# The first loads, the first value products and the issue queue of a gated attention-and-MLP kernel, reordered

## The chip, the cores and the metric

One core of one Trainium2 chip. The metric is the time of one execution on the device, in microseconds (us); lower is better. The kernel before takes 156.6 us (median of three runs, 156.52 to 161.58). "PE" is the matmul engine, "DVE" the vector engine, "ACT" the activation engine, "POOL" the GpSimd engine and "SP" the engine that issues most DMAs; "PEld" in a view is PE's loading of weights. Times inside an execution are counted from the start of the profile's span, which is about 1.7 us shorter than the time of the run.

## The reference, cut to what matters

```python
x = A_x                                              # 1 x 2048 x 448, bf16
g = sigmoid((x * gate_w).sum(-1, keepdims=True))     # gate: one column of numbers
q, k, v = split(x @ wqkv)                            # 16 heads of 28
pq, pk = q @ w_phi, k @ w_phi                        # per head
phi = concat([softmax(p), softmax(-p)])              # for p in pq, pk
kv, z = phi_k^T v, sum(phi_k)
a = (phi_q kv / (phi_q z + 1e-6)) @ wo
b = gelu(x @ w1 + b1) @ w2 + b2                      # 448 -> 1792 -> 448
return g * a + (1 - g) * b
```

## The kernel before

The kernel keeps `x` transposed in `xT`, in four blocks of 512 tokens. Blocks 1 to 3 come transposed by the DMA (`load_x`). Block 0 is loaded plainly into `x0` and transposed by PE, so that PE has work early. `WvG` holds the value weights plus one column for the gate; its last 64 rows come by a small load of their own, called **the tail** below. `Wk` and `Wq` come through transposing loads and are fused with `w_phi` on PE ("fusions", tile `w_ps`), giving `Wpk` and `Wpq`. The tiles `xS`, `WqS`, `WkS` and `WvS` are copies with the two halves of the partitions swapped, made by SBUF-to-SBUF DMAs.

The first loads:

```python
warm = w2_sb[:, 0, :]
gate = w2_sb[:, 1, :]
nc.vector.memset(w2_sb[:, 0:2, :], 0.0)          # warm and gate in one
nc.vector.memset(wphi[64:P, 3, :], 0.0)
nc.vector.memset(WvG[0:64, 3, :], 0.0)
...
for m, eng in ((0, nc.scalar), (1, nc.sync)):     # x0: a half on each queue
    eng.dma_start(x0[:, 2*m:2*m+2, :], ...)
nc.scalar.dma_start(WvG[:, 0:3, 0:D], ...)
nc.scalar.dma_start(WvG[64:P, 3, 0:D], ...)       # the tail
nc.sync.dma_start(gate[0:1, :], gate_w[None, :])  # waits for the memset
nc.scalar.dma_start(wphi[:, 0:3, :], ...)
...
load_wT(WkT, D)        # SP, transposing; SP issues in order, so after the gate
load_wT(WqT, 0)
load_x(1)
```

The start of PE's program, and the queue of swaps:

```python
dummies(8)                      # warm the clock
turn_x0(0, xp[0]); turn_gate(); turn_x0(1, xp[1])
fill_bd()
v_pair(0, on_act=True); v_pair(1)
prep(WkT, wk_at, (1, 0, 1)); prep(WqT, wq_at, (1, 0, 0))     # fusions
# SP, in this order: b1, block 2, WqS, xS(0), block 3, WkS, xS(1), WvS, w1, wo
k_pair(0); k_pair(1); ...; k_pair(2); v_pair(2); ...; k_pair(3); v_pair(3, b1=True)
for g in range(NG): q_pair(g, 0)
```

All accumulators rotate through the eight PSUM banks: three buffers "pair" and one "acc", of two banks each. A tile made earlier or later shifts the rotation of all that follow.

Of the kernel before, what the change touches and what calls it, by code (L numbers as in the profile page):

```python
# [35 lines left out]
def kernel(  # L36
# [75 lines left out]
    nc.gpsimd.memset(b1c, 0.0)  # L112
    warm = w2_sb[:, 0, :]
    gate = w2_sb[:, 1, :]
    nc.vector.memset(w2_sb[:, 0:2, :], 0.0)  # L115
    nc.vector.memset(wphi[64:P, 3, :], 0.0)
# [3 lines left out]
    x0 = oT[:, 0, 0:4 * D].rearrange("p (t d) -> p t d", t=4)  # L120
    for m, eng in ((0, nc.scalar), (1, nc.sync)):
        eng.dma_start(x0[:, 2 * m:2 * m + 2, :],
                      x[m * 256:(m + 1) * 256, :].rearrange("(t p) d -> p t d", p=P))
    nc.scalar.dma_start(WvG[:, 0:3, 0:D],
                        A_wqkv[0:384, 2 * D:3 * D].rearrange("(c p) n -> p c n", p=P))
    nc.scalar.dma_start(WvG[64:P, 3, 0:D], A_wqkv[384:448, 2 * D:3 * D])
    nc.sync.dma_start(gate[0:1, :], gate_w[None, :])
    nc.scalar.dma_start(wphi[:, 0:3, :], wphi_rows[0:384, :].rearrange("(c p) b -> p c b", p=P))
# [6 lines left out]
    def load_wT(W, base):  # L135
        nc.sync.dma_start_transpose(W[:], A_wqkv[:, base:base + NC4 * P])
# [6 lines left out]

    load_wT(WkT, D)
    load_wT(WqT, 0)
    load_x(1)
    nc.scalar.dma_start(wphi[0:64, 3, :], wphi_rows[384:448, :])


    nc.gpsimd.memset(ident[:], 1.0)  # L150
    nc.gpsimd.affine_select(out=ident[:], in_=ident[:], pattern=[[-1, P]],
# [46 lines left out]

    def v_pair(u, on_act=False, b1=False):
        v_ps = four("v_ps")  # L200
        for i in range(2):
            t = 2 * u + i
            for c in range(NC4):
                nc.tensor.matmul(v_ps[:, i, 0:D + 1], lhsT=xT[:, c, t * P:(t + 1) * P],  # L204
                                 rhs=WvG[:, c, :], start=(c == 0), stop=(c == NC4 - 1))
        if b1:
            nc.tensor.matmul(v_ps[:, 1, 480:480 + NJ], lhsT=b1c, rhs=ident[:, 0:NJ],
                             start=True, stop=True, skip_group_check=True)
        v_out(u, v_ps, slice(2 * u, 2 * u + 2), on_act)
        if b1:  # L210
            nc.vector.tensor_copy(out=b1T[:], in_=v_ps[:, 1, 480:480 + NJ])
# [117 lines left out]
    def turn_x0(m, tp):  # L329
        for i in range(2):  # L330
            for c in range(NC4):
                lo = c * P if c < 3 else 320
                nc.tensor.transpose(tp[:, c, i * P:(i + 1) * P], x0[:, 2 * m + i, lo:lo + P],  # L333
                                    ident[:])
        copy(m == 1, xT[:, :, m * 256:(m + 1) * 256], tp[:])

    def turn_gate():
        g_ps = four("g_ps")
        for c in range(NC4):
            lo = c * P if c < 3 else 320  # L340
            nc.tensor.matmul(g_ps[:, 0, c:c + 1], lhsT=gate[:, lo:lo + P], rhs=ident[:, 0:1],
                             start=True, stop=True)
        nc.vector.tensor_copy(out=WvG[:, 0:3, D], in_=g_ps[:, 0, 0:3])
        nc.vector.tensor_copy(out=WvG[HP:P, 3, D:D + 1], in_=g_ps[HP:P, 0, 3:4])

    def dummies(n):
        w_ps = four("warm_ps")
        for _ in range(n):
            nc.tensor.matmul(w_ps[:, 0, 0:D], lhsT=warm[:, 0:P], rhs=warm, start=True, stop=True)  # L349


    dummies(8)
    xp = [ps.tile([P, NC4, 256], BF16, name="xp", tag="pair", bufs=3) for _ in range(2)]
    turn[0] += 2
    turn_x0(0, xp[0])
    turn_gate()
    turn_x0(1, xp[1])
    fill_bd()
    v_pair(0, on_act=True)
    v_pair(1)  # L360
    prep(WkT, wk_at, (1, 0, 1))
    prep(WqT, wq_at, (1, 0, 0))
    def swap_w(W_S, W):
        nc.sync.dma_start(W_S[0:HP, :, :], W[HP:P, :, :])
        nc.sync.dma_start(W_S[HP:P, 0:3, :], W[0:HP, 0:3, :])

    nc.sync.dma_start(b1c[0:NJ, :], B_b1.rearrange("(j p) -> j p", p=P))
    load_x(2)
    swap_w(WqS, Wpq)
    swap_x(0)  # L370
    load_x(3)
    swap_w(WkS, Wpk)
    swap_x(1)
    swap_w(WvS, WvG)
    for f in (slice(0, F // 2), slice(F // 2, F)):
# [10 lines left out]
    k_pair(2)  # L386
    v_pair(2)
    k_norm(1)
# [152 lines left out]
```

## Time and profile before

| | kernel before |
|---|---|
| runs | 156.6, 156.52, 161.58 us |
| span of the profile | 154.4 us |
| first transpose / first value product | 4.42 / 6.18 us |
| first fusion / first keys / first queries | 9.25 / 11.14 / 20.43 us |
| first hidden unit (`hp`) / first product of the queries with `kv` and `z` (`nm`) / first output (`y`) | 43.33 / 89.75 / 90.60 us |

The starts on PE are milestones: if one is later by as much as the next, nothing was gained or lost between. The prediction shows the views. Two lines of the issue queues that I passed over also belong here. They are from the timelines of SP and of ACT (start, length of the issue, queue, line, kind, what), and show Wk's transposing load and the tail:

```profile
1.81 2.40 SPq L136 DMA_TRANSPOSE WkT<-in_A_wqkv_dram  x1
```

```profile
1.87 0.53 ACTq L126 DMA_DIRECT2D WvG<-in_A_wqkv_dram  x1
```

The two are issued 0.06 us apart, on different queues.

### The profile page before, as it was taken

The numbers are of one execution on the slowest core, as the hardware profiler recorded it, in microseconds if no ns is written. First come the engines' busy times: TensorE is split into PE (matmuls) and PEld (weight loads), VectorE is DVE, ScalarE is ACT, GpSimd is POOL, SyncE is SP. The second block draws the span as 40 slices with busy tenths as digits, with TensorE's granted clock in tenths as the row PEclk, the third lists the DMA queues.
The fourth block names the chain that finished last, engine by engine and source line by source line (L and its number), as shares of the span: only waits on it lengthen the run. The fifth ranks groups of instructions, "written<-read, shape, count | busy, mean of one in ns | idle before, by whom it ended". The sixth has DMA issues, their size and how long they took to land.

```text
span 154.4 us, 3179 instructions
## 1 busy us (share of the span) xinstructions
PE 149.4 (97%) x1303; PEld 86.6 (56%) x1303; DVE 83.2 (54%) x245; ACT 76.5 (50%) x87; POOL 32.4 (21%) x35
## 2 busy tenths in 40 slices
PE   6999999999999999999999999999999999999991
PEld 2575578666666854444444455555556555555581
DVE  3364999388891050000000059999977999977100
ACT  0559759998889527776767640111311111111121
POOL 7920489929775000000000000000000000000000
PEclk9999999999999999999999999999999999999999
DMA  4999999999993000000000001114332124334401
GB/s 151 239 213 148 213 232 254 219 222 215 218 351 135 4 0 4 0 0 4 0 0 0 4 0 34 34 39 97 93 94 64 40 64 93 81 83 38 123 30 30
DMA packets 28270, 14.91 MB, mean 97 GB/s; under 512 B 20062, under 2 KB 27872, under 8 KB 28256
## 3 DMA queue, kind: packets, MB, share of 16 engines
q1 hardware_dynamic: 27024, 14.06, 41.5%
q10 hardware_dynamic: 1232, 0.66, 1.5%
q8 instruction: 10, 0.16, 0.4%
q14 instruction: 4, 0.03, 0.1%
HBM read 6.11 MB, written 1.84 MB: 51 GB/s over the span
## 4 chain that ended last, share of the span: by engine, by line
PE 96%; DVE 1%; ACT 0%; issue 0%; ACTq 0%
PE hp L421 27%; PE y L480 27%; PE pq L303 8%; PE y L486 8%; PE nm L436 4%; PE v_ps L204 4%; PE pk L273 4%; PE v_ps L287 4%; PE pk L295 3%; PE acc L314 2%; PE warm_ps L349 2%; PE w_ps L220 1%; PE xp L333 0%; DVE xT L192 0%; ACT res L489 0%; DVE w_sb L115 0%
## 5 line engine op out<-in xcount | busy, mean ns | idle before, releaser
L480 PE MATMUL y<-w_sb,gel 128*128 128x448 bf16 (+1 forms) x238 | 45.2, 341 | 0.0
L421 PE MATMUL hp<-xT,w_sb 64*128 64x512 bf16 x196 | 42.7, 376 | 0.0
L421 PE MATMUL hp<-xS,w_sb 64*128 64x512 bf16 x196 | 42.3, 376 | 0.0
L426 ACT ACTIVATE gel<-hp,b1T 128x1024 bf16<-128x1024 f32 x28 | 30.8, 1110 | 13.0 <-PE hp L421 13.0
L489 ACT ACTIVATE res<-y,ungate 128x448 bf16<-128x448 f32 (+1 forms) x17 | 10.4, 611 | 50.4 <-PE y L486 50.3
L480 PEld LDWEIGHTS <-gel 128*128 128x128 bf16 x238 | 23.1, 98 | 19.0
L421 PEld LDWEIGHTS <-w_sb 64*128 64x128 bf16 x392 | 20.6, 94 | 21.5
L264 POOL TENSOR_TENSOR phik<-phik,rec 128x1792 bf16<-128x1792 bf16 (+1 forms) x8 | 25.0, 3127 | 15.0 <-DVE rec L261 15.0
L441 DVE COPY st<-nm 128x32 f32<-128x32 f32 x32 | 4.5, 183 | 35.6 <-PE nm L436 35.6
L457 DVE TENSOR_TENSOR tmp<-nm,al 128x448 bf16<-128x448 f32 x32 | 18.4, 616 | 0.0
L259 DVE TENSOR_REDUCE sums<-phik 128x64 f32<-128x1792 bf16 x8 | 16.0, 2005 | 2.6 <-ACT phik L252 2.6
L486 PE MATMUL y<-wo_sb,oT 128*128 128x448 bf16 (+1 forms) x68 | 14.7, 341 | 0.0
L303 PE MATMUL pq<-xT,Wpq 64*128 64x512 bf16 x56 | 13.6, 376 | 0.0
L303 PE MATMUL pq<-xS,WqS 64*128 64x512 bf16 x56 | 12.0, 376 | 0.0
L192 DVE CAST vaug<-v_ps 128x896 bf16<-128x896 f32 x7 | 7.5, 1073 | 4.7 <-PE v_ps L287 3.2
L308 ACT ACTIVATE EqP<-pq 128x1024 bf16<-128x1024 f32 x8 | 8.3, 1040 | 3.4 <-PE pq L303 3.4
L309 ACT ACTIVATE EqN<-pq 128x1024 bf16<-128x1024 f32 x8 | 8.3, 1042 | 0.0
L436 PE MATMUL nm<-KVbd,EqP 128*128 128x120 bf16 x64 | 8.3, 216 | 0.0
L436 PE MATMUL nm<-KVbd,EqN 128*128 128x120 bf16 x64 | 8.3, 216 | 0.0
L251 ACT ACTIVATE phik<-pk 128x896 bf16<-128x896 f32 x8 | 7.5, 941 | 1.4 <-PE pk L273 1.4
L486 PEld LDWEIGHTS <-oT 128*128 128x128 bf16 x68 | 6.1, 98 | 3.3
L252 ACT ACTIVATE phik<-pk 128x896 bf16<-128x896 f32 x8 | 7.6, 949 | 0.0
(87 smaller groups left out, 147.7 us busy)
## 6 DMA issues: line engine op xcount, KB each, us to landing
w_sb<-in_B_w_dram SPq DMA_DIRECT2D x4, 784.0 KB, 14.2
out_dram<-res SPq DMA_DIRECT2D x15, 112.0 KB, 1.9
w_sb<-in_B_w_dram SPq DMA_DIRECT2D x1, 1568.0 KB, 17.4
xS<-xT SPq DMA_DIRECT2D x2, 256.0 KB, 4.0
xS<-xT SPq DMA_DIRECT2D x2, 192.0 KB, 4.3
WvG<-in_A_wqkv_dram ACTq DMA_DIRECT2D x1, 336.0 KB, 4.2
wo_sb<-in_A_wo_dram SPq DMA_DIRECT2D x1, 336.0 KB, 17.4
WqS<-Wpq SPq DMA_DIRECT2D x1, 256.0 KB, 4.2
```

The source lines that it names most:

```text
L259: nc.vector.reduce_sum(out=sums[:], in_=ph, axis=AX.X)
L264: eng.tensor_tensor(out=ph[:, lo:hi], in0=ph[:, lo:hi], in1=rec[:, lo:hi, :, None].to_broadcast([P, hi - lo, 2, DH]), op=ALU.mult)
L303: nc.tensor.matmul(pq[:, i, :], lhsT=w_half(Wpq, WqS, i, k)[:, g * P:(g + 1) * P], rhs=x_half(i, k, h), start=(k == 0), stop=(k == NK - 1))
L308: nc.scalar.activation(out=EqP[:, g, dst], in_=src, func=ACT.Exp)
L309: nc.scalar.activation(out=EqN[:, g, dst], in_=src, func=ACT.Exp, scale=-1.0)
L421: nc.tensor.matmul(hp[:, i, :], lhsT=w1_sb[i * HP:(i + 1) * HP, k, j * P:(j + 1) * P], rhs=x_half(i, k, h), start=(k == 0), stop=(k == NK ...
L426: nc.scalar.activation(out=gel[h][:, j, :], in_=hp[:].rearrange("p a b -> p (a b)"), func=ACT.Gelu_apprx_tanh, bias=b1T[:, j:j + 1])
L436: nc.tensor.matmul(nm[s][:, g * 2 * KW:(g + 1) * 2 * KW], lhsT=E[:, g, tok], rhs=KVbd[:, g, s, :], start=True, stop=True)
L457: nc.vector.tensor_tensor(out=tmp[:, s, :].rearrange("p (x h d) -> p x h d", x=NPR, h=2), in0=nmv[s][:, :, 0:PW].rearrange("p x (h d) -> p ...
L480: nc.tensor.matmul(y, lhsT=gel[t // 8][:, j, (t % 8) * P:(t % 8 + 1) * P], rhs=w2_sb[:, j, cols], start=(j == 0), stop=False)
L486: nc.tensor.matmul(y, lhsT=oT[:, c, tok], rhs=wo_sb[:, c, cols], start=False, stop=(c == NC4 - 1))
L489: nc.scalar.activation(out=res[:, cols], in_=y, func=ACT.Copy, scale=ungate[:, t:t + 1])
```

## The change

The intent is to feed the first value product sooner: half of `x0` and `Wv` go first, the rest of `x0` follows and is transposed inside the first value pair, block 1 is multiplied while `Wq` is still on its way, and `WvS` and `xS` are swapped earlier because nothing holds them up.

```diff
-    warm = w2_sb[:, 0, :]
+    warm = w2_sb[:, 0, 0:P]
-    nc.vector.memset(w2_sb[:, 0:2, :], 0.0)
+    nc.vector.memset(warm, 0.0)
+    nc.vector.memset(gate, 0.0)
...
-    for m, eng in ((0, nc.scalar), (1, nc.sync)):
-        eng.dma_start(x0[:, 2 * m:2 * m + 2, :], ...)
-    nc.scalar.dma_start(WvG[:, 0:3, 0:D], ...)
+    nc.scalar.dma_start(x0[:, 0:2, :], ...)
+    nc.sync.dma_start(WvG[:, 0:3, 0:D], ...)
     nc.scalar.dma_start(WvG[64:P, 3, 0:D], ...)
+    nc.scalar.dma_start(x0[:, 2:4, :], ...)
     nc.sync.dma_start(gate[0:1, :], gate_w[None, :])
...
     load_wT(WkT, D)
+    load_x(1)
     load_wT(WqT, 0)
-    load_x(1)
+    nc.scalar.activation(out=first[:], in_=warm[0:1, 0:1], func=ACT.Exp)
...  # gate casts from DVE to ACT; all copies of transposes on DVE;
...  # the dummies: one PSUM tile for all, 512 columns by repeating warm
-    dummies(8)
+    dummies(7)
     turn_x0(0, xp[0])
     turn_gate()
-    turn_x0(1, xp[1])
+    dummies(1)
+    v_pair(0, on_act=True, between=lambda: turn_x0(1, xp[1]))
     fill_bd()
-    v_pair(0, on_act=True)
     v_pair(1)
     prep(WkT, wk_at, (1, 0, 1))
+    v_pair(2)
     prep(WqT, wq_at, (1, 0, 0))
...
+    swap_w(WvS, WvG)
+    swap_x(0)
     load_x(2)
     swap_w(WqS, Wpq)
-    swap_x(0)
     load_x(3)
     swap_w(WkS, Wpk)
     swap_x(1)
-    swap_w(WvS, WvG)
...
     k_pair(2)
-    v_pair(2)
```

More of the change, by code (lines that the diff above doesn't have):

```diff
@@ L120 @@
     x0 = oT[:, 0, 0:4 * D].rearrange("p (t d) -> p t d", t=4)
-    for m, eng in ((0, nc.scalar), (1, nc.sync)):
-        eng.dma_start(x0[:, 2 * m:2 * m + 2, :],
-                      x[m * 256:(m + 1) * 256, :].rearrange("(t p) d -> p t d", p=P))
-    nc.scalar.dma_start(WvG[:, 0:3, 0:D],
-                        A_wqkv[0:384, 2 * D:3 * D].rearrange("(c p) n -> p c n", p=P))
+    nc.scalar.dma_start(x0[:, 0:2, :], x[0:256, :].rearrange("(t p) d -> p t d", p=P))
+    nc.sync.dma_start(WvG[:, 0:3, 0:D],
+                      A_wqkv[0:384, 2 * D:3 * D].rearrange("(c p) n -> p c n", p=P))
     nc.scalar.dma_start(WvG[64:P, 3, 0:D], A_wqkv[384:448, 2 * D:3 * D])
+    nc.scalar.dma_start(x0[:, 2:4, :], x[256:512, :].rearrange("(t p) d -> p t d", p=P))
     nc.sync.dma_start(gate[0:1, :], gate_w[None, :])
@@ L144 @@
     load_wT(WkT, D)
+    load_x(1)
     load_wT(WqT, 0)
-    load_x(1)
     nc.scalar.dma_start(wphi[0:64, 3, :], wphi_rows[384:448, :])
+    first = consts.tile([1, 1], F32, name="first")
+    nc.scalar.activation(out=first[:], in_=warm[0:1, 0:1], func=ACT.Exp)
     nc.gpsimd.memset(ident[:], 1.0)
@@ L197, in v_out, with v_pair @@
         copy(on_act, lg[:, tiles], v_ps[:, :, D])
-    def v_pair(u, on_act=False, b1=False):
+    def v_pair(u, on_act=False, b1=False, between=None):
         v_ps = four("v_ps")
@@ L202, in v_pair @@
             t = 2 * u + i
+            if i == 1 and between is not None:
+                between()
             for c in range(NC4):
@@ L334, in turn_x0 @@
                                     ident[:])
-        copy(m == 1, xT[:, :, m * 256:(m + 1) * 256], tp[:])
+        copy(False, xT[:, :, m * 256:(m + 1) * 256], tp[:])
     def turn_gate():
@@ L342, in turn_gate @@
                              start=True, stop=True)
-        nc.vector.tensor_copy(out=WvG[:, 0:3, D], in_=g_ps[:, 0, 0:3])
-        nc.vector.tensor_copy(out=WvG[HP:P, 3, D:D + 1], in_=g_ps[HP:P, 0, 3:4])
+        nc.scalar.copy(out=WvG[:, 0:3, D], in_=g_ps[:, 0, 0:3])
+        nc.scalar.copy(out=WvG[HP:P, 3, D:D + 1], in_=g_ps[HP:P, 0, 3:4])
+    w_ps = four("warm_ps")
     def dummies(n):
-        w_ps = four("warm_ps")
         for _ in range(n):
-            nc.tensor.matmul(w_ps[:, 0, 0:D], lhsT=warm[:, 0:P], rhs=warm, start=True, stop=True)
-    dummies(8)
+            nc.tensor.matmul(w_ps[:, 0, :], lhsT=warm, rhs=warm[:, None, :].to_broadcast([P, 4, P]),
+                             start=True, stop=True)
+    dummies(7)
     xp = [ps.tile([P, NC4, 256], BF16, name="xp", tag="pair", bufs=3) for _ in range(2)]
```

## The prediction

> **What bounds the kernel now.** First I read the page's busy shares and slices, then the chain that ended last, then the start of the timeline by engine, because everything the change moves lies before 29 us.
>
> The page of the kernel before: busy shares, then the slices.
>
> ```profile
> PE 149.4 (97%) x1303; PEld 86.6 (56%) x1303; DVE 83.2 (54%) x245; ACT 76.5 (50%) x87; POOL 32.4 (21%) x35
> ...
> DMA  4999999999993000000000001114332124334401
> ```
>
> The matmul engine PE is busy for 149.4 of 154.4 us, so at most 5 us of the span hold no matmul. The chain puts 96% on PE. DMA engines are full too, but only for the first 12 slices (to about 46 us). So whatever moves the time has to change PE's work, or its idle time, or its clock before the second product.
>
> The waits of PE, then its timeline up to the first query pair (start, length, engine, line, what, idle before it).
>
> ```profile
> PE warm_ps L349 <- DVE w_sb L115: 1.5, 1, 1.5
> PE v_ps L204 <- DVE WvG L343: 0.3, 1, 0.3
> ```
>
> ```profile
> 1.46 3.17 PE L349 MATMUL warm_ps<-w_sb 128*128 128x448 bf16 x8 [1.46 <-DVE w_sb L115]
> 4.42 0.89 PE L333 MATMUL xp<-ident,oT 128*128 128x128 bf16 x8
> ...
> 5.25 0.61 PE L333 MATMUL xp<-ident,oT 128*128 128x128 bf16 x8
> 6.18 3.04 PE L204 MATMUL v_ps<-WvG,xT 128*128 128x449 bf16 x15 [0.33 <-DVE WvG L343]
> ...
> 9.25 1.09 PE L220 MATMUL w_ps<-w_sb,WkT 128*128 128x140 bf16 x16
> 10.18 1.13 PE L220 MATMUL w_ps<-w_sb,WqT 128*128 128x140 bf16 x16
> 11.14 4.76 PE L273 MATMUL pk<-Wpk,xT 128*128 128x448 bf16 x24
> ...
> 20.43 0.39 PE L303 MATMUL pq<-xT,Wpq 64*128 64x512 bf16 x1
> ```
>
> PE's only waits are 1.46 us at the start and 0.33 us at 6.18; the rest of the 5 us is the tail after 151 us. From 6.18 on it streams: 16 value matmuls by 9.25 (0.192 us each), 16+16 fusions by 11.14 (0.059 each). No wait on x0's load shows, so loading it sooner gains nothing by itself.
>
> The second thing to see is the issue queue SP, which feeds PE from 20 us on.
>
> ```profile
> 13.54 0.57 SPq L364 DMA_DIRECT2D WqS<-Wpq  x1
> 14.15 1.06 SPq L365 DMA_DIRECT2D WqS<-Wpq  x1
> 15.26 0.65 SPq L141 DMA_DIRECT2D xS<-xT  x1
> 15.96 0.62 SPq L142 DMA_DIRECT2D xS<-xT  x1
> ...
> 23.00 0.90 SPq L364 DMA_DIRECT2D WvS<-WvG  x1
> 23.94 0.72 SPq L365 DMA_DIRECT2D WvS<-WvG  x1
> ```
>
> SP issues without a pause from 1.8 to 32 us. The tile view of xS gives up to 4.6 us from issue to landing: the copy issued at 15.96 lands at 20.52 by its completion records. The first query matmul that reads xS starts at 20.57. WvS, issued at 23.94 and 4.2 us under way, lands at 28.04 to 28.14; the first matmul that reads it starts at 28.15, though its partner started at 27.80. So the queue is just in time twice, and costs PE about 0.1 us at 20.5 and 0.35 us at 27.8.
>
> **What the Trainium skill says.**
> - "TensorE: Matmul & The Clock Gate", Part 1: PE runs at half clock until about 3.4 us of sustained activity, in a free-running window. The trace agrees: dummies of 448 columns are 0.373 us apart, later matmuls 0.19; the spacing of the transposes drops from 0.107 to 0.056 us at about 4.95, 3.5 us after PE's start.
> - The same page, Part 4, says transposes don't reach the full clock. The trace differs: the second eight are 0.055 us apart.
> - "VectorE: DVE Perf Modes", Zero memsets can be issued as uint32: one cycle per element whatever the width. The trace agrees: 448 elements 0.43 us, 224 0.24 us, 14 0.07 us.
> - "DMA: Bandwidth & Descriptors", Issuing engines are not separate DMA queues: loads from two queues share the same engines. The trace agrees: SP's and ACT's halves of x0 both land by 3.98.
>
> **The change, part by part.**
> 1. *Start.* The memset before the dummies shrinks from 448 to 128 columns, 64 words: by the row of 14 words (0.07) and that of 224 (0.24), about 0.11 us instead of 0.43. PE starts at 0.97+0.11+0.05 = 1.13. Seven dummies of 512 columns at half clock take 7 x 0.427 = 2.99 us, as the eight of 448 did (8 x 0.373 = 2.98). Transposes start at about 4.1, not 4.42: 0.3 us sooner. x0's first half now shares the engines with Wv in place of x0's second half, so it lands as before, by about 3.9.
> 2. *Fewer things before the first value matmul.* Only four transposes of each of two tiles (8 in all) and the gate go first. With the clock rising at 4.65 to 5.0 they end at 5.1 to 5.2; the vector copy takes 0.69; 0.14 more passes to the first value matmul (6.04 to 6.18 before). It starts at 5.95 to 6.05. The gate's two copies go to ACT and no longer follow that copy on the vector engine. **Gain 0.15 to 0.2 us.** The one dummy after the gate fills idle time.
> 3. *Transposes inside the first value pair.* The 8 other transposes (8 x 0.055 = 0.44 us) used to fill PE's wait; now they stand in its stream. First tile to 6.76, transposes to 7.2, second tile to 7.96. The copy of those transposes can only start at 7.4 and end at 8.1, so the second pair starts at about 8.22 where it started at 7.72. The two pairs end at 9.75, not 9.25: **loss of about 0.5 us**, already net of 1 and 2.
> 4. *Block 1's values between the fusions.* The same 8 matmuls, 1.53 us, move from 15.74 to about 10.7. Nothing is saved on PE but a stall: the first keys waited 0.3 us of weight load for the last piece of Wpk, about 0.06 to 0.1 us of it on PE; now 1.5 us lie between. The load order (Wk, block 1, Wq) fits this: the transposes so far landed at 8.05, 9.87 and 12.2; block 1 takes the middle place and lands by about 10.3, wanted at 10.7; Wq by about 12.0, wanted at 12.2. **Gain 0.1.**
> 5. *Swaps reordered.* WvS (0.90+0.72 = 1.6 us of issue) goes ahead of the copies that the queries need. The last of these is now WqS instead of xS. Adding up issue times from 9.85: b1 0.5, WvS 1.5, xS 1.3, block 2 2.75 and WqS up to 1.06 in; its second part is issued at about 16.5 and lands 3.5 to 4.4 us later, at 20 to 21. Queries are wanted at 20.43+0.5-0.1-0.1 = 20.75. So **loss of 0 to 0.5**. In return WvS is no longer awaited at 27.8: **gain 0.3**; xS's second pair, issued at about 22.5, lands at 26.5 to 27, and is wanted at 26.8.
> 6. *First exponential early.* The table load (1.28 us at 3.61) was already beside the dummies. No change.
>
> Sum: +0.5 -0.1 -0.1 -0.3 + (0 to 0.5) = 0 to +0.5 us. Later stages have the same PE work and carry any shift to the end. The time before is 156.6, so about **156.8**.
>
> **The rivals.**
> (a) *The start really shortens.* If the aim holds (first values sooner, no stall behind the second copy, every transfer in time), the steps give -0.2 at the first value, -0.1 and -0.4 later, with the transposes still costing 0.44: at best about 156.2. For it: the waits at 20.5 and 27.8 are real. Against it: no wait for x0 shows, and PE's work is the same.
> (b) *The queue becomes the bound.* 393 KB of WvS ahead of WqS delays the queries in full. Successive swaps landed 0.75 to 1.3 us apart after 16 us, so the pair costs 1.7 us: 20.5 becomes 22.2, a PE wait of 1.5, less 0.3: about 158. For it: DMA share full throughout. Against it: DMA traffic fell to a trickle twice before, around 11.8 and from 14.8 to 15.5, so there is slack before 16 us.
> (c) *The clock gate.* The window runs freely; if it closes late the transposes and the first value matmuls run at half clock, +0.2 to +1.5. Against: 2.99 us of dummies start sooner than before, and PE hardly stops.
> (d) *ACT becomes the bound* from 22 to 33 us, where it is continuously busy (windows view: 5.00 of 5.00 from 25 to 30). PE has four accumulator buffers and about 0.8 us of slack, so a shift passes on one for one and isn't enlarged.
>
> **Range and chances.** Steps 3, 4 and 5 give 0 to +0.5; (a) makes -0.4, (b) up to +1.4, and fast runs of the kernel before differ by 0.1 to 0.5. I take 156.1 to 157.7. Two per cent is 3.1 us, more than any rival makes: chances faster 0.01, within 2% 0.97, slower 0.02 (a slow state or several rivals together).
>
> **What will show it.** PE's first dummy at about 1.13 (step 1); first value matmul near 6.0 (step 2); 8 transposes between two groups of four value matmuls and a wait of about 0.3 us for the vector copy before the second pair (step 3); fusions at 9.75 and no wait of keys on Wpk (step 4); first query matmul between 20.7 and 21.3, and whether it waits for WqS; none for WvS at 28 (step 5); first hidden-layer matmul, at 43.33 before, 0 to 0.5 later. I am wrong if queries start after 22 (rival b), if block 1 or Wq land late and PE waits at 10.7 or 12.2, or if hidden layers start before 43.1.

## The result

| | before | after |
|---|---|---|
| runs, us | 156.6, 156.52, 161.58, 159.69 | 161.42, 162.02, 160.87, 162.07 |
| median | 158.14 | 161.72 |
| span of the profile | 154.4 | 159.7 |

The ratio of the fast runs is 1.032, with a 95% interval of 1.025 to 1.040: slower. A ratio here is the mean time of one kernel's fast runs over that of the other's fast runs of the same rounds, so it isn't quite the ratio of the medians that I quote. "Slow" runs, those more than 1.5% above the fastest of the same kernel, are left out; two of the four runs of the kernel before were such. The slow runs of the kernel before are as long as the normal runs of the changed one. That was a clue.

The busy shares and slices of the page of the changed kernel:

```profile
PE 152.2 (95%) x1303; PEld 80.8 (51%) x1303; DVE 83.5 (52%) x245; ACT 76.0 (48%) x89; POOL 32.1 (20%) x35
...
PE   7399999999999999999999999999999999999991
...
PEclk9857999999999999999999999999999999999999
```

PE is busy for 152.2 us instead of 149.4, with the same 1303 matmuls. The granted clock (PEclk, tenths of full speed) fell to 0.5 to 0.8 in the second to fourth slices, and PE was busy for only three tenths of the second. Where it waited, and its timeline:

```profile
PE xp L337 <- DMA oT<-in_A_x_dram: 2.7, 2, 2.4
PE warm_ps L354 <- DVE w_sb L115: 1.1, 1, 1.1
PE v_ps L208 <- DVE xT L194: 0.3, 1, 0.3
PE y L486 <- ACT gel L432: 0.3, 1, 0.3
```

```profile
1.06 3.00 PE L354 MATMUL warm_ps<-w_sb 128*128 128x512 bf16 x7 [1.06 <-DVE w_sb L115]
6.49 0.62 PE L337 MATMUL xp<-ident,oT 128*128 128x128 bf16 x8 [2.44 <-DMA oT<-in_A_x_dram]
...
7.90 1.68 PE L208 MATMUL v_ps<-WvG,xT 128*128 128x449 bf16 x4 [0.34 <-DVE xT L194]
9.82 1.04 PE L337 MATMUL xp<-ident,oT 128*128 128x128 bf16 x8 [0.24 <-DMA oT<-in_A_x_dram]
10.65 4.11 PE L208 MATMUL v_ps<-WvG,xT 128*128 128x449 bf16 x12
14.60 1.09 PE L224 MATMUL w_ps<-w_sb,WkT 128*128 128x140 bf16 x16
```

A new wait, 2.44 us for the first half of `x0`, stands before the transposes (`x0` lies in the tile `oT`). After it the clock is taken back: four value products take 1.68 us instead of 0.93 (they start 0.37 us apart and not 0.19), and so it stays until about 14 us. The clock records in the trace put the half clock at 7.17 to 13.99, 6.83 us. It is 6.83 us in e1 and e7 (below) too, after waits of 4.2 and 3.2 us: in these three kernels the stretch lost was the same, whatever the length of the wait. The milestones show where the 5.3 us lie:

| first ... (us) | before | after | difference |
|---|---|---|---|
| transpose | 4.42 | 6.49 | +2.07 |
| value product | 6.18 | 7.90 | +1.72 |
| fusion | 9.25 | 14.60 | +5.35 |
| keys (block 1's 1.5 us now lie ahead) | 11.14 | 17.98 | +6.84 |
| queries (block 1 is done in both) | 20.43 | 25.67 | +5.24 |
| hidden unit | 43.33 | 48.41 | +5.08 |
| `nm` | 89.75 | 94.66 | +4.91 |
| output `y` | 90.60 | 95.94 | +5.34 |

Everything is lost before the first fusion. The first value product is 1.72 us late. The value pairs then take 6.70 us instead of 3.07, which I split into about 13 products at half clock (13 x 0.18 = 2.3), eight transposes now in the stream at half clock (0.85), and waits for the rest.

Why was `x0` late? The first issues of ACT in the changed kernel, then of SP:

```profile
0.80 0.49 ACTq L122 DMA_DIRECT2D oT<-in_A_x_dram  x1
1.32 0.55 ACTq L125 DMA_DIRECT2D WvG<-in_A_wqkv_dram  x1
1.91 0.59 ACTq L126 DMA_DIRECT2D oT<-in_A_x_dram  x1
```

```profile
0.80 0.46 SPq L123 DMA_DIRECT2D WvG<-in_A_wqkv_dram  x1
...
1.75 2.97 SPq L136 DMA_TRANSPOSE WkT<-in_A_wqkv_dram  x1
```

The first half of `x0` is issued as early as before, at 0.80, but its last completion record comes at 6.45 instead of 3.98. The second half, now issued at 1.91, lands at 9.78. Wk's transposing load is issued at 1.75 and takes 2.97 us to issue. SP then stands until 6.46: its load of block 1 waits 1.7 us for the first half of `x0` (SP's waits; in the trace the two loads signal on the same semaphore). So a late `x0` also holds back block 1 and Wq.

### The profile page after: what moved, and what is told of

Same layout as the page of the kernel before. It is cut to its first block, busy times and chain, and to the rows that moved or that the text cites. A ratio compares the mean times of both kernels' runs of the same rounds, so it can differ in the third digit from the quotient of the medians.

```text
span 159.7 us, 3185 instructions
## 1 busy us (share of the span) xinstructions
PE 152.2 (95%) x1303; PEld 80.8 (51%) x1303; DVE 83.5 (52%) x245; ACT 76.0 (48%) x89; POOL 32.1 (20%) x35
## 3 DMA queue, kind: packets, MB, share of 16 engines
HBM read 6.11 MB, written 1.84 MB: 50 GB/s over the span
## 4 chain that ended last, share of the span: by engine, by line
PE 91%; DMA 5%; ACT 1%; ACTq 1%; issue 0%
PE y L486 27%; PE hp L427 27%; PE pq L307 8%; PE y L492 8%; DMA oT<-in_A_x_dram 5%; PE v_ps L208 4%; PE pk L277 4%; PE nm L442 4%; PE v_ps L291 3%; PE pk L299 3%; PE acc L318 2%; PE w_ps L224 1%; ACT gel L432 1%; PE xp L337 1%; ACTq L125 0%; ACTq L122 0%
## 5 line engine op out<-in xcount | busy, mean ns | idle before, releaser
L427 PEld LDWEIGHTS <-w_sb 64*128 64x128 bf16 x392 | 18.9, 94 | 23.2
L307 PE MATMUL pq<-xT,Wpq 64*128 64x512 bf16 x56 | 12.9, 376 | 0.0
L307 PE MATMUL pq<-xS,WqS 64*128 64x512 bf16 x56 | 12.9, 376 | 0.0
L208 PE MATMUL v_ps<-WvG,xT 128*128 128x449 bf16 x32 | 9.2, 444 | 0.3 <-DVE xT L194 0.3
## 6 DMA issues: line engine op xcount, KB each, us to landing
wo_sb<-in_A_wo_dram SPq DMA_DIRECT2D x1, 336.0 KB, 16.5
```

Source lines behind the costliest of these rows:

```text
L208: nc.tensor.matmul(v_ps[:, i, 0:D + 1], lhsT=xT[:, c, t * P:(t + 1) * P], rhs=WvG[:, c, :], start=(c == 0), stop=(c == NC4 - 1))
L307: nc.tensor.matmul(pq[:, i, :], lhsT=w_half(Wpq, WqS, i, k)[:, g * P:(g + 1) * P], rhs=x_half(i, k, h), start=(k == 0), stop=(k == NK - 1))
L427: nc.tensor.matmul(hp[:, i, :], lhsT=w1_sb[i * HP:(i + 1) * HP, k, j * P:(j + 1) * P], rhs=x_half(i, k, h), start=(k == 0), stop=(k == NK ...
```

## The experiments

All kernels gave correct results. Runs sent together ran on one chip, beside the kernel before; its fast medians lie between 156.4 and 156.6 us on all of the chips.

### First batch: which part makes the loss?

I had three theories. *Load order*: with Wv in front, `x0` comes late because it shares the DMA engines with Wv. *Neighbour*: the loads that are issued beside Wk's transposing load are held up by it, so Wk's place decides. *Clock*: the wait itself is short, and the lost clock costs the most.

**e1_loads_back**: the changed kernel with the old loads of `x0` and `Wv`.

```diff
-    nc.scalar.dma_start(x0[:, 0:2, :], ...)
-    nc.sync.dma_start(WvG[:, 0:3, 0:D], ...)
+    for m, eng in ((0, nc.scalar), (1, nc.sync)):
+        eng.dma_start(x0[:, 2 * m:2 * m + 2, :], ...)
+    nc.scalar.dma_start(WvG[:, 0:3, 0:D], ...)
     nc.scalar.dma_start(WvG[64:P, 3, 0:D], ...)
-    nc.scalar.dma_start(x0[:, 2:4, :], ...)
```

> The changed kernel with the four loads of x0 and Wv put back as they were (both halves of x0 first, one on each queue; Wv behind on ACT), all else as changed. If the load order is the cause (either by Wv sharing the engines with x0 or by the transposing load of Wk running beside x0), the first transposes start at about 4.1 us instead of 6.5, the clock is never withdrawn again, and the time is 156 to 157.5 us: my prediction's steps 2 to 5 are then tested without the failed one. If something else of the change is the cause (block 1's values between the fusions, the swaps), the time stays above 160.

**e2_loads_only**: the reverse, the kernel before with the new loads of `x0` and `Wv` alone.

```diff
-    for m, eng in ((0, nc.scalar), (1, nc.sync)):
-        eng.dma_start(x0[:, 2 * m:2 * m + 2, :], ...)
-    nc.scalar.dma_start(WvG[:, 0:3, 0:D], ...)
+    nc.scalar.dma_start(x0[:, 0:2, :], ...)
+    nc.sync.dma_start(WvG[:, 0:3, 0:D], ...)
     nc.scalar.dma_start(WvG[64:P, 3, 0:D], ...)
+    nc.scalar.dma_start(x0[:, 2:4, :], ...)
```

> The kernel before with only the four loads of x0 and Wv reordered as in the change. If the load order alone is the cause, x0's first half lands at about 6.4 us and its second near 9.8 and the time is 160 us or more (both halves are wanted before any value matmul, so even a little worse than the changed kernel). If the cause needs the rest of the change, the time stays near that of the kernel before, 156.5 to 158.

**e3_wk_held**: the changed kernel, with Wk's load (and so all later ones of SP) held until both halves of `x0` have landed, by two copies of one element from `x0` into the tile that Wk's load overwrites.

```diff
-    load_wT(WkT, D)
-    load_x(1)
-    load_wT(WqT, 0)
...
+    nc.vector.tensor_copy(out=WkT[0:1, 0, 0:1], in_=x0[0:1, 0, 0:1])
+    nc.vector.tensor_copy(out=WkT[0:1, 0, 1:2], in_=x0[0:1, 2, 0:1])
+    load_wT(WkT, D)
+    load_x(1)
+    load_wT(WqT, 0)
```

> The changed kernel with Wk's transposing load (and those behind it) held until both halves of x0 have landed. Theory T (the transposing load runs beside x0 and holds up its completion): x0's first half lands at 4.0 to 4.8 us and its second at 5.0 to 6, although Wv still shares the engines. Rival S (sharing with Wv, or the load of ACT starting late, is what delays x0): the first half still lands after 6 us. Wk itself comes late here, at 10 to 12 us, so the whole time says less: 157 to 160 under T, above 161 under S.

**e4_more_dummies**: the changed kernel with 19 and 4 dummies instead of 7 and 1, so that PE stays busy through the waits.

```diff
-    dummies(7)
+    dummies(19)
...
-    dummies(1)
+    dummies(4)
```

> The changed kernel with 19 dummies instead of 7 ahead of x0 and 4 instead of 1 behind the gate, so that the matmul engine doesn't stop while it waits for x0. If the clock's withdrawal is a loss of its own, 12 value matmuls at 0.374 instead of 0.19 us and 8 transposes at 0.107 instead of 0.056, about 2.6 us come back: 158.5 to 159.5 us. If x0's lateness is all of the loss, the time stays within 0.7 us of the changed kernel.

Measured (three of the seven runs of the kernel before in this batch were slow, at 161.1 to 161.5, so the intervals are wide):

| | median, us | ratio to before (95%) | first value / fusion / queries, us |
|---|---|---|---|
| e1_loads_back | 162.03 | 1.036 (1.030 to 1.041) | 9.54 / 15.64 / 26.72 |
| e2_loads_only | 162.37 | 1.037 (1.031 to 1.044) | 10.99 / 15.65 / 26.83 |
| e3_wk_held | 161.46 | 1.032 (1.030 to 1.035) | 7.21 / 11.85 / 24.27 |
| e4_more_dummies | 160.88 | 1.028 (1.026 to 1.031) | 7.90 / 12.07 / 23.16 |

**e1 and e2 together are the surprise.** The loads alone make the whole loss, and with the old loads the rest of the change makes the whole loss too. So the load order can't be the one cause. The landings in e1 say what comes late there: both halves of `x0` land at 4.09 and 3.83 as in the kernel before, but the tail, 57 KB issued at 1.88, lands at 9.21 (5.83 before), and the first value product waits for it. In e1 the gate's memset is done sooner than in the kernel before, because the change has made the memset ahead of it short; so Wk's load is issued at 1.73 instead of 1.81, 0.15 us ahead of the tail instead of 0.06.

**e3 bears out the neighbour for the second half of `x0`, and for the first half in part.** With Wk held to 6.16, all plain loads land by 6.32, and the second half of `x0`, issued at 1.91 as before, at 5.96 instead of 9.78. But Wk then lands at 10.87 and Wq at 15.60; PE waits 0.9 us for Wq and 1.0 for `WqS`, and the gain is gone again. The first half of `x0` lands at 5.34 there instead of 6.45, but not at 3.98: that rest is not Wk's doing. It lies between the two theories of the expectation, and the total is above 161, where rival S had it.

**e4 shows the clock's share and where it went.** The transposes still start at 6.49, but the value products run at full clock and the fusions start at 12.07 instead of 14.60: 2.5 us gained. Its largest waits on PE were these:

```profile
PE nm L442 <- ACT gel L432: 1.2, 1, 1.2
PE warm_ps L354 <- DVE w_sb L115: 1.1, 1, 1.1
PE pq L307 <- DMA WqS<-Wpq: 1.0, 1, 1.0
```

The queries now wait for `WqS`, which the changed order of swaps puts after block 2, and `nm` has a wait of 1.2 us that no other kernel had. It comes with a shift of the PSUM rotation: in the kernel's compiled allocation the last hidden unit lies in bank 4, where `nm` wants to go (bank 2 in the kernel before, no wait; bank 0 in the changed kernel, which the first `y` wants: its wait of 0.3 above). Part of the lateness of `WqS` is SP's own wait: it stands 1.8 us here for the first half of `x0`. As to the banks, e4 makes no tile sooner; more matmuls into the dummies' tile were enough to shift the rotation. Only 0.8 us of the 2.5 reached the end, so the total missed the expectation (158.5 to 159.5). This makes the clock a real part of the loss, but a consequence of the late load.

### Second batch: a few tenths of a microsecond of Wk's issue, and nothing else

SP issues in order, and the gate's row waits for a memset on DVE. So the order of three memsets moves Wk's issue, with no other change to the program. Five rounds.

**e5_before_wk_later** (the kernel before) and **e7_before_wk_sooner** (the kernel before):

```diff
 # e5: Wk issued at 2.51
-    nc.vector.memset(w2_sb[:, 0:2, :], 0.0)
+    nc.vector.memset(warm, 0.0)
     nc.vector.memset(wphi[64:P, 3, :], 0.0)
     nc.vector.memset(WvG[0:64, 3, :], 0.0)
+    nc.vector.memset(gate, 0.0)
```

```diff
 # e7: Wk issued at 1.72
-    nc.vector.memset(w2_sb[:, 0:2, :], 0.0)
+    nc.vector.memset(gate, 0.0)
+    nc.vector.memset(warm, 0.0)
```

> The kernel before, whose runs fall at either 156.4 or 161 us, with one small edit: the memset of the gate row, for which SP's queue waits before it issues Wk's transposing load, moves behind two other memsets, so that Wk's load is issued at about 2.5 us instead of 1.81, after ACT's last piece of Wv (1.87). Theory R (a race: whichever plain load is issued after Wk's transposing load crawls beside it until about 9 us, and in the kernel before 0.06 us decide it): all runs at 156.3 to 157.5, none near 161. Rival N (the two times come from outside, memory or clock noise): both times still appear, about half and half.

> The kernel before with the same memset split and put first, so that Wk's transposing load is issued at about 1.65 us instead of 1.81 and the dummies start when they did. Theory R: the last piece of Wv now always comes behind it and lands after 8 us, and all runs take 160.5 to 162. Rival N: both times appear as in the kernel before. Were the earlier load itself a gain, the runs would be at 156.3 or less.

**e6_after_wk_later** is the changed kernel with the gate's memset after WvG's (Wk at 2.35). **e8_loads_back_wk_later** is the same with the old loads of `x0` and `Wv` (the diff of e1).

```diff
     nc.vector.memset(warm, 0.0)
-    nc.vector.memset(gate, 0.0)
     nc.vector.memset(wphi[64:P, 3, :], 0.0)
     nc.vector.memset(WvG[0:64, 3, :], 0.0)
+    nc.vector.memset(gate, 0.0)
```

> The changed kernel with Wk's load issued at about 2.5 us instead of 1.75, after the second half of x0 (1.91). Theory R: x0's halves land at about 5.3 and 6 us as they did with Wk held, and the time falls to 157.5 to 159 (x0's first half still shares the engines with Wv and comes 1.4 us later than before). Rival N: x0's second half lands near 9.8 and the time stays at 161 to 162.

> The changed kernel with x0's and Wv's loads as they were and Wk's load issued at about 2.5 us. Theory R: no load lies behind Wk's, x0 lands by 4.1 and the last piece of Wv by 6, and what remains are steps 2 to 5 of my prediction: 156.2 to 157.5 us in all runs. If block 1's values between the fusions or the reordered swaps cost something of their own, the time stays above 158.

| | runs | median (range), us | ratio (95%) |
|---|---|---|---|
| before | 11 | 156.42 (155.94 to 156.79, one of 160.92) | 1 |
| e5, Wk at 2.51 | 6 | 156.29 (156.25 to 156.49) | 1.000 (0.999 to 1.002) |
| e7, Wk at 1.72 | 6 | 161.11 (160.25 to 161.63) | 1.030 (1.027 to 1.033) |
| e6 | 5 | 159.38 (158.98 to 159.72) | 1.020 (1.018 to 1.022) |
| e8 | 5 | 158.76 (158.55 to 159.01) | 1.016 (1.014 to 1.018) |

The landings, by the last completion record of each load (issue in brackets):

| us | Wk issued | tail | first half of x0 | second half of x0 | Wk lands |
|---|---|---|---|---|---|
| before | 1.81 | 5.83 (1.87) | 3.98 (0.81) | 3.72 (0.80) | 8.05 |
| e5 | 2.51 | 5.74 (1.87) | 4.07 (0.80) | 3.79 (0.80) | 7.72 |
| e7 | 1.72 | **8.51** (1.87) | 4.04 (0.80) | 3.75 (0.80) | 9.37 |
| after | 1.75 | 7.12 (1.32) | **6.45** (0.80) | **9.78** (1.91) | 10.38 |
| e6 | 2.35 | 5.40 (1.32) | 5.25 (0.80) | 6.88 (1.92) | 8.73 |

In e5 and e7 the tail is issued at the same time, 1.87. With Wk's transposing load issued 0.15 us ahead of it, it lands 2.8 us later than with Wk 0.64 behind it. Wk itself lands later too, though it was issued sooner. In the windows of e5 (stretch, length, then busy time of PE, PEld, DVE, ACT and POOL, granted clock, DMA share, GB/s; the DMA share adds up the time of all packets, so it can exceed 1) and the same of e7, the core's transfers are slower:

```profile
5.00:6.00 1.00, 0.40 (x10) 0.43 (x11) 0.66 (x2) 0.00 (x0) 0.86 (x4) 1.00 1.25 242
6.00:7.00 1.00, 1.00 (x11) 0.62 (x9) 0.94 (x5) 0.66 (x1) 0.85 (x4) 1.00 1.26 263
7.00:8.00 1.00, 1.00 (x7) 0.50 (x6) 0.31 (x2) 0.48 (x2) 0.94 (x5) 1.00 1.29 247
```

```profile
5.00:6.00 1.00, 0.64 (x14) 0.56 (x12) 0.69 (x1) 0.41 (x2) 0.86 (x4) 1.00 1.19 169
6.00:7.00 1.00, 0.00 (x0) 0.00 (x0) 0.00 (x0) 0.69 (x1) 0.85 (x4) 1.00 1.34 174
7.00:8.00 1.00, 0.00 (x0) 0.00 (x0) 0.00 (x0) 0.00 (x0) 0.94 (x5) 0.98 1.44 170
```

The last two columns are the point: the engines are as busy in e7 (1.19 to 1.44 against 1.25 to 1.29) but move 169 to 174 GB/s against 242 to 263. (The kernel before, in its fast run, moved 172, 254 and 214.) PE's timeline of e5, then of e7, shows what it makes of it:

```profile
6.14 3.23 PE L205 MATMUL v_ps<-WvG,xT 128*128 128x449 bf16 x16
9.21 1.09 PE L221 MATMUL w_ps<-w_sb,WkT 128*128 128x140 bf16 x16
```

```profile
8.86 6.11 PE L205 MATMUL v_ps<-WvG,xT 128*128 128x449 bf16 x16 [3.22 <-DVE WvG L344]
14.80 1.09 PE L221 MATMUL w_ps<-w_sb,WkT 128*128 128x140 bf16 x16
```

The tail is late by 2.8 us, PE waits 3.22 us for the cast into WvG that needs it, loses the clock, and runs the 16 value products at half speed: 6.11 us instead of 3.23. Together that is the 5.6 us between the fusions, of which 4.8 reach the end. So **the kernel before, with Wk's load issued 0.09 us sooner, is as slow as the changed kernel**. The gate's row, which e7 also issues sooner (1.33), is not the cause: e14 below issues it at 1.33 with Wk at 2.34, and its tail lands at 5.81.

Two limits of this. Not every load that is under way is held up: in e7 both halves of `x0`, issued at 0.80, land at 4.04 and 3.75 as in e5, while in the changed kernel the first half, issued as early, lands at 6.45 instead of e6's 5.25. And it isn't the order alone: the kernel before issues Wk 0.06 us ahead of the tail and most of its runs are fast, e2 issues it 0.11 us ahead of the second half of `x0` and all of its runs are slow.

This also gives a meaning to its slow runs. Over all jobs, 7 of its 44 runs were slow, with a mean of 160.9 us; e7 has 161.0, and in e5, with Wk 0.64 us behind the tail, none of six was. The kernel before issues the two loads 0.06 us apart, so it seems to sit on the edge. I have no trace of one of its slow runs, so that this is what happened in them is inferred and not shown.

e6 and e8 take the head start away in the changed kernel: 161.72 becomes 159.38 in e6, so 2.3 us are the neighbour's (with its share of the clock and of SP's wait). Both are above what was expected of them (157.5 to 159, and 156.2 to 157.5). The loads with Wv in front cost another 0.6 (e6 against e8): the first half of `x0` then lands at 5.25 and not at 3.94. In the windows view from 2 to 3 us, DMA moved 87 GB/s in the changed kernel and 264 before, so Wv in front starts slowly. Why, no run shows. After both, 2.3 us to the kernel before remain.

PE's waits in e8, the largest first, say where to look next:

```profile
PE warm_ps L355 <- DVE w_sb L115: 1.1, 1, 1.1
PE pq L308 <- DMA WqS<-Wpq: 0.9, 1, 0.9
PE g_ps L346 <- DMA w_sb<-in_gate_w_dram: 0.6, 1, 0.6
PE w_ps L225 <- DMA WqT<-in_A_wqkv_dram: 0.4, 1, 0.4
PE y L487 <- ACT gel L433: 0.3, 1, 0.3
```

### Third batch: the rest, one part after the other

The waits for `WqS` and `Wq` point at the swaps (step 5 of the prediction) and at block 1's place (step 4). The wait of 0.3 at `y` points at the banks.

**e9_swaps_back**: e8 with the old order of swaps.

```diff
-    swap_w(WvS, WvG)
-    swap_x(0)
     load_x(2)
     swap_w(WqS, Wpq)
+    swap_x(0)
     load_x(3)
     swap_w(WkS, Wpk)
     swap_x(1)
+    swap_w(WvS, WvG)
```

> The 158.76 us version (changed kernel, loads of x0 and Wv as before, Wk's load after all of them) with the swaps in their old order. If the queue order of the swaps is what made the queries wait for WqS (1.2 us there), the second part of WqS lands by 21.5 us, the queries don't wait, a wait of about 0.3 for WvS comes back near 29, and the time falls by 0.7 to 1.1 us, to 157.7 to 158.1. If the queue as a whole is the bound, the wait only moves to another tensor and the time stays within 0.3 us of 158.76.

**e10_swaps_v2_back**: e9 with block 1 as before, too.

```diff
     load_wT(WkT, D)
-    load_x(1)
     load_wT(WqT, 0)
+    load_x(1)
...
     prep(WkT, wk_at, (1, 0, 1))
-    v_pair(2)
     prep(WqT, wq_at, (1, 0, 0))
...
     k_pair(2)
+    v_pair(2)
```

> As the run before, with block 1's values and the load order Wk, Wq, block 1 as in the kernel before too. What is left of the change is x0's second half turned within the first value pair, the smaller memset and the 512-wide dummies. My step 3 says 0.5 us slower than the kernel before at the fusions, and the accumulator banks cost another 0.4 near 93 us: 157.0 to 157.5. Without a loss from step 3 it would be 156.3 to 156.8.

**e11_banks_mended**: e8, with the one dummy after the gate replaced by four transposes into the next tile of transposes. The dummies' tile is then free sooner, and the rotation of the banks is that of the kernel before.

```diff
-    dummies(1)
+    for _ in range(4):
+        nc.tensor.transpose(xp[1][:, 0, 0:P], warm, ident[:])
```

> The 158.76 us version with the one dummy behind the gate replaced by four transposes into the accumulator that x0's second half will use, so that the accumulators rotate through the banks as they did in the kernel before (the last hidden unit no longer sits in the bank that the first output tile needs). If that bank is the cause of the 0.48 us step before the first output tile, it goes back to about 0.05 and the time falls by 0.3 to 0.45 us, to 158.3 to 158.5; otherwise 158.76 as it is.

**e12_all_before_wk**: the kernel before with everything that the first value pair needs issued ahead of Wk: the gate's memset first, the tail on SP between the gate and Wk, b1's load and the gate's casts on ACT.

```diff
-    nc.vector.memset(w2_sb[:, 0:2, :], 0.0)
+    nc.vector.memset(gate, 0.0)
+    nc.vector.memset(warm, 0.0)
...
-    nc.scalar.dma_start(WvG[64:P, 3, 0:D], ...)
     nc.sync.dma_start(gate[0:1, :], gate_w[None, :])
+    nc.sync.dma_start(WvG[64:P, 3, 0:D], ...)
...
+    nc.scalar.dma_start(b1c[0:NJ, :], ...)
...
-        nc.vector.tensor_copy(out=WvG[:, 0:3, D], in_=g_ps[:, 0, 0:3])
+        nc.scalar.copy(out=WvG[:, 0:3, D], in_=g_ps[:, 0, 0:3])
...  # the second cast likewise
```

> A candidate from the kernel before: the last piece of Wv goes through SP's queue between the gate row and Wk, so that all plain loads that the first values need come ahead of the transposing load; b1's load leaves SP's queue for ACT's; the gate's two copies go to ACT. If the race theory holds, all runs are in the fast mode; the first value matmul comes at about 5.7 instead of 6.18 and the queue is about 0.5 us further on at the queries: 155.6 to 156.2 us. If any later load crawls beside Wk's, some runs are above 158.

| | median (range), us | ratio (95%) |
|---|---|---|
| before, none of 11 slow | 156.60 (156.26 to 156.95) | 1 |
| e9 | 159.32 (158.75 to 159.45) | 1.017 (1.015 to 1.019) |
| e10 | 157.49 (156.89 to 159.0) | 1.007 (1.004 to 1.011) |
| e11 | 158.62 (158.21 to 158.88) | 1.013 (1.011 to 1.015) |
| e12 | 157.20 (157.05 to 158.76) | 1.005 (1.003 to 1.008) |

**e9 is inconclusive.** Its clock had not risen when the values began: four products took 1.69 us at 6.24, and the fusions started at 11.64 instead of e8's 9.86. Those 1.8 us cover what the swaps did. The start depends on the gate's row, which landed about when PE ran out of work (waits of 0.6 us in e9, 1.0 in e11, 1.2 in e10), so this whole batch has an uncertain start. **e11** shows what it was for: from `nm` to `y` took 0.85 us instead of 1.28, as in the kernel before, and the wait at `y` is gone; its total is only 0.14 below that of e8, which ran on another chip; its first fusion was 0.5 us later than e8's. **e12 is a miss**, for a reason of its own: it has no early exponential, so the table load of ACT sat at 6.04 to 7.32, just ahead of the gate's cast that needed it, and the first value product came at 7.56.

### Fourth batch: the parts undone one by one, on a mended start

To settle the terms of the sum, I made the start firm in all kernels of one batch: `x0` as before, the tail on SP between the gate and Wk (so ahead of Wk by program order), and twelve transposes in place of the one dummy, which hold the clock and put the banks right. Each kernel undoes one more part of the change. Five rounds.

**e14_change_race_free**: the changed kernel with that start (Wk issued at 2.34, the tail at 1.73). All else of the change is in it.

```diff
-    nc.scalar.dma_start(x0[:, 0:2, :], ...)
-    nc.sync.dma_start(WvG[:, 0:3, 0:D], ...)
-    nc.scalar.dma_start(WvG[64:P, 3, 0:D], ...)
-    nc.scalar.dma_start(x0[:, 2:4, :], ...)
+    for m, eng in ((0, nc.scalar), (1, nc.sync)):
+        eng.dma_start(x0[:, 2 * m:2 * m + 2, :], ...)
+    nc.scalar.dma_start(WvG[:, 0:3, 0:D], ...)
     nc.sync.dma_start(gate[0:1, :], gate_w[None, :])
+    nc.sync.dma_start(WvG[64:P, 3, 0:D], ...)
...
-    dummies(1)
+    for _ in range(12):
+        nc.tensor.transpose(xp[1][:, 0, 0:P], warm, ident[:])
```

> The changed kernel made free of the race in another way (x0's halves first as before, Wv's last piece through SP's queue ahead of Wk's transposing load, the gate row loaded early), with the accumulator banks mended and 12 short transposes instead of one dummy so that the clock holds. What is left against the kernel before: x0's second half within the first value pair, block 1 between the fusions, and the swaps. From the 158.76 version less 0.43 for the banks: 158.0 to 158.5.

**e15_and_swaps_back**: e14 and the diff of e9.

> The run before with the swaps in their old order as well. The difference of the two is the cost of putting WvS ahead in the queue: 0.7 to 1.1 us if the queries' wait for WqS (1.1 us of it) is its own loss and the wait for WvS (0.3) comes back, so 157.1 to 157.6; under 0.3 us of difference if the queue as a whole is the bound and the wait only moves to another tensor. The trial of this in the 158.76 version said nothing, because the clock fell there.

**e16_and_block1_back**: e15 and the diff of e10.

> The run before with block 1's values and the load order Wk, Wq, block 1 as in the kernel before too. The difference is the cost of the wait for Wq (0.4 to 0.8 us where it was seen) less the little that the keys' stall was worth: 0.3 to 0.6 us, so 156.7 to 157.2.

**e17_x0_back_too**: e16, and the second half of `x0` transposed before the first value pair again.

```diff
-    for _ in range(12):
-        nc.tensor.transpose(xp[1][:, 0, 0:P], warm, ident[:])
-    v_pair(0, on_act=True, between=lambda: turn_x0(1, xp[1]))
+    turn_x0(1, xp[1])
+    v_pair(0, on_act=True)
```

> The run before with x0's second half turned ahead of the first value pair again. Step 3 of my prediction says that turning it within the pair costs 0.5 us at the fusions; then this takes 156.0 to 156.5, in all runs, with nothing left of the change but the smaller memset, the wider dummies, the early table load and the gate's copies on ACT. If it is under the fast runs of the kernel before by more than 0.3 us, those small parts are a gain of their own.

| | median (range), us | ratio (95%) | step |
|---|---|---|---|
| before | 156.58 (156.12 to 156.79, one of 160.73) | 1 | |
| e14 | 158.28 (158.0 to 158.76) | 1.011 (1.010 to 1.013) | |
| e15 | 157.86 (157.76 to 157.98) | 1.009 (1.007 to 1.010) | swaps: -0.4 |
| e16 | 156.61 (156.45 to 156.94) | 1.001 (0.999 to 1.002) | block 1: -1.3 |
| e17 | 156.17 (156.09 to 156.55) | 0.998 (0.997 to 1.000) | x0 in the pair: -0.4 |

Each part of the change that reached this batch was a loss. The swaps' 0.4 is the least certain: the two kernels' runs hardly part (158.0 to 158.76 against 157.76 to 157.98), and their profiled runs took the same time, though e14's fusions start 0.27 us sooner. The largest is block 1's place, twice the expected 0.3 to 0.6. SP's timelines of e15, then of e16, show one part of the reason:

```profile
12.03 1.26 SPq L134 DMA_TRANSPOSE xT<-in_A_x_dram  x1
15.63 0.51 SPq L373 DMA_DIRECT2D WqS<-Wpq  x1
```

```profile
11.95 1.26 SPq L134 DMA_TRANSPOSE xT<-in_A_x_dram  x1
13.43 0.50 SPq L372 DMA_DIRECT2D WqS<-Wpq  x1
```

With block 1 between the fusions, the queries' fusion comes later, so `Wpq` is ready later, and the in-order queue stands at `WqS` from 13.29 to 15.63. All that is behind it comes later: `WvS` lands at 29.97 instead of 28.18, and the second `xS` pair at 28.14 instead of 26.41. The first group of keys and of values that read them take 1.57 and 1.85 us on PE in e15, 1.32 and 1.34 in e16: 0.8 us. The other part is `Wq` itself, which block 1 overtook: it landed at 12.87 in e14, and PE waits for it (0.5 us in e14, 0.3 in e15, none in e16). In this pair of profiles another 0.2 us is the start: e15's tail landed at 6.07 and e16's at 5.89.

e17 keeps only small parts of the change (the shorter memsets, fewer and wider dummies, the gate's casts on ACT, the early table load and the copies on DVE) and the mended start. Its values start late, at 6.36, but stand in one piece:

```profile
6.36 3.23 PE L209 MATMUL v_ps<-WvG,xT 128*128 128x449 bf16 x16 [1.20 <-ACT WvG L348]
9.43 1.09 PE L225 MATMUL w_ps<-w_sb,WkT 128*128 128x140 bf16 x16
```

In e16 they started 0.15 us sooner (6.21) and the fusions 0.49 later (9.92). The twelve transposes went out with the same edit, but PE stood idle before the values in both kernels (0.59 and 1.20 us), so they were not on the path. e17 is 0.2% below the kernel before (0.3 to 0.4 us), the lowest of all that I tried; which of the parts that it keeps gives this, no run shows. None of its six runs was slow. At 7 slow runs in 44, six fast ones by chance alone have a probability of (37/44)^6 = 0.35, so that doesn't prove by itself that the second mode is gone; e5's six, e16's six and e14's and e15's nine point the same way. But slow runs came unevenly, and in the two batches of these kernels only 2 of 22 runs of the kernel before were slow; at that rate all 27 fast by chance has (20/22)^27 = 0.08.

## Why the prediction was wrong, by its own steps

The prediction was 156.8 us with a range to 157.7; the changed kernel took 161.7.

**The step that failed is in step 1: "x0's first half now shares the engines with Wv in place of x0's second half, so it lands as before, by about 3.9."** It landed at 6.45. Two things were wrong in it. First, its neighbours were not only Wv: Wk's transposing load, issued at 1.75, held up both halves of `x0`. With Wk at 2.35 (e6) they land at 5.25 and 6.88 instead of 6.45 and 9.78, which is worth 2.3 us of the changed kernel's time; e5 against e7 shows the same on the tail. Second, even without that, with Wv in front, it lands at 5.25 (5.34 in e3) and not at 3.9, for 0.6 us at the end (e6 against e8). The same step counted as a gain that the memsets shrink. They also moved Wk's issue from 1.81 to 1.75 or 1.73, and with the old loads that was enough for the whole loss (e1). About the second half of `x0`, issued at 1.91 and landed at 9.78, I made no step at all.

**Rival (c), the clock**, was part of the loss, but by another cause: not a window that closes late, but a wait of 2.4 us on PE. Its size was up to 1.5; in e4, dummies through the wait gained 2.5 us at the fusions and 0.8 at the end. My "PE hardly stops" rested on the failed step.

| step of the prediction | predicted | measured |
|---|---|---|
| 1, PE's first dummy | 1.13 | 1.06, nearly right |
| 1, transposes | 4.1 | 6.49; 4.02 in e8 and e14, where the loads come in time |
| 2, first value product | 5.95 to 6.05 | 7.90; 6.13 to 6.15 in e14 and e8, held by the tail or the gate |
| 3, x0 inside the pair | loss of 0.5 | 0.44 (e16 against e17), right |
| 4, block 1 between the fusions | gain of 0.1 | loss of 1.3 (e15 against e16) |
| 5, swaps | loss of 0 to 0.5, gain of 0.3 | loss of 0.4 net (e14 against e15) |
| 6, early exponential | no change | right for this kernel; without it, gate casts on ACT wait for the table (e12) |
| not in it: PSUM banks | - | `nm` to `y` 1.28 instead of 0.85 |

Step 4 failed at "Wq by about 12.0, wanted at 12.2": it landed at 12.81 in e8 and 12.87 in e14. I also didn't see that `Wpq` gates the queue. In step 5 I let `WqS` be issued at about 16.5 and land at 20 to 21; in e8 it was issued at 18.30 and landed at 22.77. The issues of block 2 took 2.13 and 2.30 us there, beside the swaps, where I had used 1.45 and 1.26. Rival (b) named that mechanism; e8 waits 0.9 us for `WqS` where it had 1.5. In the changed kernel itself steps 4 and 5 cost nothing that shows: no wait for `Wq` or `WqS` is among PE's waits, because the start was so late that the queue had caught up. They come to light only when the start is mended, as in e4, e6 and e8.

From the changed kernel down, each number is from one of the kernels above, on three chips whose fast medians of the kernel before agree within 0.2 us:

| | us | what was undone |
|---|---|---|
| after | 161.7 | |
| e6 | 159.4 | Wk's head start: 2.3 |
| e8 | 158.8 | Wv in front: 0.6 |
| e14 | 158.3 | banks, gate and filler: 0.5 (other chip, three edits) |
| e15 | 157.9 | swaps: 0.4 |
| e16 | 156.6 | block 1: 1.3 |
| e17 | 156.2 | x0 in the pair: 0.4 |

Two of its sums were loose as well, without bearing on the result. Rival (a)'s own terms (-0.2, -0.1, -0.4, +0.44) give -0.26, so 156.3 and not 156.2; and the range ends at 157.7, below rival (b)'s "about 158".

The **chances** failed with the step: 0.02 for slower. A sign was there before the prediction. One of the three runs of the kernel before took 161.58 us, 3% more than the others, on a single core, and I counted it as a slow state that has nothing to do with the kernel. It could have been read as an event in the program that is decided by a hair, though no trace of it was at hand to say in which stretch.

What stays open: how a transposing load slows plain loads beside it, and why 0.06 us of head start is mostly harmless and 0.11 is not; why loads with Wv in front move so little between 2 and 3 us; and what a slow run of the kernel before looks like inside.

## What to carry to other kernels

Let the plain loads that the first products need go out ahead of the first transposing load, by program order on one queue and not by a few hundredths of a microsecond between two; and when a kernel has two distinct times, look for the two issues that stand nearly level before calling it noise. A long wait on the matmul engine in the first 15 us can cost twice: after waits of 2.4 to 4.2 us (the changed kernel, e7, e1) the clock was at half for 6.83 us, while after waits of 1.2 us in e10 and e17 the products ran at full clock. And a part that seems free while the start is late may be the next bound: judge it on a kernel whose start is mended.

## What the Trainium skill lacked or had wrong

- "DMA: Bandwidth & Descriptors", Rules for kernel authors, says in its row on two transposing DMAs that "A transpose next to ordinary DMAs needs nothing". For the data this agrees (all outputs were right); for the time it doesn't. A 57 KB plain load issued at 1.87 us landed at 5.74 with the transposing load issued at 2.51, and at 8.51 with it issued at 1.72; meanwhile the core's DMA moved 170 GB/s instead of 250. The order of issue across two engines was worth 4.8 us of 156 here (e5 and e7), and the page has nothing on that.
- No page that I read says that the profile's granted clock doesn't show the first rise; it belongs to "TensorE: Matmul & The Clock Gate", Part 1, which warns only in general that a trace's clock events can be unreliable. In the windows view of the kernel before it read 1.00 from 2 to 3 us, where the dummies ran 0.373 us apart, and in that of e9 from 6 to 8 us, where four value products took 1.69 us instead of 0.93. The spacing of the matmuls shows it.
- No page that I read warns that one PSUM tile made sooner, or given more matmuls (e4), shifts the rotation of all later ones. Here it moved a wait to `y` (0.3 us, step of 1.28 instead of 0.85) or to `nm` (1.2 us in e4), 85 us after the edit.
- "TensorE: Matmul & The Clock Gate", Part 4, says that the full clock doesn't engage for transposes. The runs bear out what the prediction read in the trace: eight transposes take 0.62 us in e17 and 1.03 in e9, where the clock was at half. Whether transposes alone would raise the clock, no run here tests.
